# Five places for the first eight pieces of words, and no preparing step ahead of the first gated row

## The chip, the cores and the metric

The kernel runs on one core of one Trainium2 chip. The metric is the device time of one execution in microseconds (us). A profile comes from one execution, whose span is a little different from the timed runs.

## The reference

Two blocks stand behind each other, all in float32. The first is attention over hash buckets, with 4 batches, 8 heads, 768 tokens and 64 numbers a head. The second is a feed-forward block with a gate, on 3072 tokens of 512 numbers, with 1536 hidden ones.

```
q_bits = (q @ proj > 0);  k_bits = (k @ proj > 0)        # 6 bits each
mask   = bucket(q_bits)[:, None] == bucket(k_bits)[None, :]
scores = where(mask, q @ k.T / sqrt(D), -1e9)
attn   = exp(scores - max) / (sum + 1e-9)
x      = (attn @ v), heads side by side                  # (3072, 512)
out    = (silu(x @ w_gate) * (x @ w_val)) @ w_out
```

The weights w_gate, w_val and w_out come in as float64, and the kernel reads them as pairs of 32-bit words.

## The kernel before

**Attention.** Two heads make a pair, and a batch has four pairs. A pair is worked on in two half-units of 384 queries, and a half-unit in six units, one for each chunk of 128 keys. `score` multiplies queries and keys on TensorE (PE), adds the bits of the hash by a second product, and lets ScalarE (ACT) take the exponential (L458). `attend` (L469) multiplies the result with v. `add` (L483, L487) sums the exponentials on VectorE (DVE); `total` (L500, L508, L513) turns the sum into a reciprocal and spreads it by DMA from SyncE's queue (SP); `norm` (L520) applies it. `front` prepares the next pair: transposes of k and q (L377 on PE for the first pairs, L420 on DVE for later ones), and hash products (L394, L402), whose signs ACT takes (L387) and DVE scales (L389).

**Gated rows.** From the unit `LATE`, which is the first half-unit of batch 1, the feed-forward of the batch before runs in between: after the scores and `attend` of a half-unit PE works on one gated row. There are six such rows in a batch, numbered 0 to 5 here, and each has 14 steps: seven products of Strassen's scheme, each for gate (g = 0) and value (g = 1). They use three banks of PSUM, a, b and c, for each of the two, out of seven that scores and other products share in turn. A product is copied from its bank by ACT (L607) or added to a tile by DVE (L548); ACT takes the tanh (L530), DVE finishes gate (L531) and product (L535). Before row 0 DVE makes eight sums of the inputs (L548, `xc` and `xT`). In row 0 the products go in the order 0, 3, 1, 2, 4, 5, 6, so the product that DVE adds at once (number 3, called A12) is the second one. After the six rows come the output products (`po`, L544, with sums at L548).

**Words.** The float64 weights arrive in 36 pieces of 512 KB: 24 of the gate and value weights in turns of four, and 12 of w_out. Each needs a *place* in SBUF until it is narrowed to float32. The list `homes` says which: `early` and `middle` are two sets of four places inside `hid`, the tile which later holds the hidden values of the rows; `beside` and `late` are inside `room`, which also holds weights, sums and some exponentials; `None` takes one of two own buffers (`words`). `load_words` issues the DMA of a piece (L263, from GpSimd's queue, POOL, the first two from SP), a few pieces ahead of the one being narrowed:

```
        for i in range(len(words), len(pieces)):
            if i - done > (6 if 8 <= i < 28 else 4):
                break
```

A DMA into a place which was used before waits, in the issuing queue, until the piece before it there is narrowed; what stands behind it in the queue waits as well.

**Preparing steps.** Narrowing a piece takes two ACT instructions (L278, L279, called by `scale_to`, ahead of need) and three DVE instructions: L292, L294 and L297. Each DVE instruction is one *preparing step*. After four pieces of the gate and value weights `form` takes four steps more (L326, sums of Strassen's scheme), and writes blocks to DRAM from POOL's queue (`ram`, L318, L320, L329). `bring` (L308, POOL) reads a block back for the row that needs it, in two parts. After the last piece, twelve steps (L349) combine the rows of w_out. There are 144 steps from piece 0 on. `prepare_on(n)` takes n of them, and the main loop says where: so many after each half-unit, and then so many for each step of a gated row, with `part` counting the steps of the row:

```
        prepare_on(4)
        if half == 1 and n >= NP:
            total(n)
        prepare_on(0 if LATE - NCH <= u <= LATE else 3)
        ...
            if part < 9:
                prepare_on(size)
```

The order of every engine's instructions is the order in which the program writes them. Nothing is moved by a scheduler.

Of the kernel before, what the change touches and what calls it, by code (L numbers as in the profile page):

```python
# [18 lines left out]
def kernel(  # L19
# [175 lines left out]
    def part(size, at=None, **dims):  # L195
        at = taken[0] if at is None else at
        taken[0] = at + size
        if len(dims) == 0:
            return room[:, at : at + size]
        ((axis, length),) = dims.items()  # L200
        return room[:, at : at + size].rearrange(f"p (n {axis}) -> p n {axis}", **dims)
# [42 lines left out]
    def as_words(t):  # L244
        return t.bitcast(I32).rearrange("p (f w) -> p f w", w=2)

    spots = [hid[:, half, m].rearrange("p f q -> p (f q)") for half in range(2) for m in range(2)]
    early = [as_words(t[:, 0 : 2 * PIECE]) for t in spots]
    middle = [as_words(t[:, NFP // 2 * HQ : NFP // 2 * HQ + 2 * PIECE]) for t in spots]
    late = [as_words(part(2 * PIECE, at=stage_at + i * 2 * PIECE)) for i in range(4)]  # L250
    beside = as_words(part(2 * PIECE, at=down_at + 8 * BL))
    turn = [None] * 2 + [beside]
    homes = [(early + middle)[i % 8] for i in range(12)]
    homes += middle + turn + middle + turn + late + turn + late[:3]

    def load_words(done, queue=nc.gpsimd):
        for i in range(len(words), len(pieces)):
            if i - done > (6 if 8 <= i < 28 else 4):
                break
            words[i] = homes[i]  # L260
            if words[i] is None:
                words[i] = wraw.tile([P, PIECE, 2], I32, tag="words", name="words")
            queue.dma_start(words[i].rearrange("p f w -> p (f w)"), pieces[i][1])  # L263
# [18 lines left out]
    def scale_ahead():  # L282
        scale_to(min(progress["piece"] + 4, progress["scaled"] + 1))
# [70 lines left out]
    def prepare_on(n):  # L354
        for _ in range(n):
            next(preparing, None)
# [84 lines left out]
    LATE = NP * 2 * NCH  # L441
# [5 lines left out]
    def score(u):  # L447
        n, half, c = units[u]
        qs = slice(half * HQ, (half + 1) * HQ)
        ks = slice(c * P, (c + 1) * P)  # L450
        sc = [bank("sc")[:, 0:HQ] for _ in range(2)]
        for x, start in ((T, True), (bits, False)):
            for h in range(2):
                rows = slice(h * D, (h + 1) * D)
                nc.tensor.matmul(sc[h], x["k", n][rows, ks], x["q", n][rows, qs],  # L455
                                 start=start, stop=not start)
        for h in range(2):
            nc.scalar.activation(weights(u)[:, h, 0:HQ], sc[h], AF.Exp, scale=SCALE)  # L458

    def attend(u):  # L460
        n, half, c = units[u]
        b, pr = pairs[n]
        a = weights(u)
        if c == 0:
            av[n] = av_ps.tile([P, 512], FP32, tag="av", name="av")
        ps = av[n]
        width = AW if half == 0 else HQ
        for h in range(2):
            nc.tensor.matmul(ps[h * D : (h + 1) * D, 0:width], raws["v", n][:, h, c, :],  # L469
                             a[:, h, 0:width], start=c == 0, stop=c == NCH - 1)  # L470
        if c == NCH - 1:
            if half == 0:
                xT[b, pr] = xp.tile([P, S], FP32, tag="xT", name="xT")
                mean[n] = att.tile([P, 1], FP32, tag="e", name="e")
                nc.scalar.activation(mean[n], ps[:, HQ : HQ + 1], AF.Copy, scale=EPS)
            nc.scalar.copy(xT[b, pr][:, half * HQ : (half + 1) * HQ], ps[:, 0:HQ])

    def add(u):
        n, half, c = units[u]
        a = weights(u)  # L480
        if c == 1:
            acc[n, half] = att.tile([P, 2, HQ], FP32, tag="acc", name="acc")
            nc.vector.scalar_tensor_tensor(out=acc[n, half], in0=weights(u - 1)[:, :, 0:HQ],  # L483
                                           scalar=S * EPS / P, in1=a[:, :, 0:HQ],
                                           op0=ALU.add, op1=ALU.add)
        elif c > 1:
            nc.vector.tensor_tensor(acc[n, half], acc[n, half], a[:, :, 0:HQ], op=ALU.add)  # L487

    def total(n):

        b, pr = pairs[n]

        ps = av_ps.tile([P, 512], FP32, tag="av", name="sum") if b == 0 else bank("sum")
        t = [acc.pop((n, half)) for half in range(2)]
        for h in range(2):
            for half in range(2):
                g = (2 * h + half) * BLOCK
                nc.tensor.matmul(ps[g : g + BLOCK, 0:HQ], ones, t[half][:, h, :],  # L500
                                 start=True, stop=True)
        if b == 0:
            space = wo.rearrange("p f m -> p (f m)")
            space = space[:, n % 2 * 3 * HQ : (n % 2 + 1) * 3 * HQ].rearrange("p (x q) -> p x q", q=HQ)
            r, t = space[:, 2, :], space[:, 0:2, :]
        else:
            r, t = t[1][:, 0, :], t[0]
        nc.vector.reciprocal(r, ps[:, 0:HQ])  # L508
        for half in range(2):
            for h in range(2):  # L510
                g = (2 * h + half) * BLOCK
                for at in (h * D, h * D + BLOCK):
                    nc.sync.dma_start(t[at : at + BLOCK, half, :], r[g : g + BLOCK, :])  # L513
        waiting.append(lambda: norm(n, t))
        if pr == NP - 1:
            push_ffn(b)
# [200 lines left out]
    def prepare_pair(count):  # L717
        for _ in range(count):
            rest.extend(f for f in steps.pop(0)() or [] if f)

    def finish(todo):
        while todo:
            todo.pop(0)()
# [5 lines left out]
    for u in range(0, N, NCH):  # L729
        n, half, _ = units[u]  # L730
        gating = u >= LATE
        if u == MOVE:
            progress["late"] = True
            for t in late_ring:
                nc.gpsimd.memset(t[:, :, HQ:AW], 1.0)
        for c in range(NCH):
            score(u + c)
            if u == 0 and c in (0, 1, 2, 4):
                prepare_pair(1)
                finish(rest)  # L740
            if c == 1 and half == 0 and 0 < n <= NP:
                total(n - 1)
            if c:
                add(u + c)
        if n <= NP:
            finish(waiting)
        if not gating and half == 0:
            steps = front(n + 1)
        if not gating and u > 0:
            prepare_pair(2)  # L750
        for _ in range(1 if u else 2):
            scale_ahead()
        for c in range(NCH):
            attend(u + c)
        if not gating:
            scale_ahead()
        if half == 1 and n + 2 < len(pairs):
            load(n + 2)
        if not gating:
            prepare_pair(2 if u > 0 else 4)  # L760
        finish(first)
        finish(rest)
        prepare_on(4)
        if half == 1 and n >= NP:
            total(n)
        prepare_on(0 if LATE - NCH <= u <= LATE else 3)
        if not gating:
            continue
        chores = []
        if n + 1 < len(pairs):  # L770
            if half == 0:
                steps = front(n + 1)
                chores = [None, steps.pop(0), None, steps.pop(0)]
            else:
                chores = [None, steps.pop(0)]

        credit += 14 if n < 2 * NP else 15.75
        end = True
        part = 0
        while atoms and (credit > 0 or not end):  # L780
            size, atom, end = atoms.pop(0)
            credit -= size
            atom()
            part += size
            if part >= 11 or u + NCH == N and part >= 6:
                finish(waiting)
                if u + NCH == N:
                    finish([first.pop(0) for _ in range(min(2, len(first)))])
            if part < 9:
                prepare_on(size)  # L790
            if 6 < part < 11 or u == LATE and part > 10:
                scale_ahead()
            for _ in range(size):
                if chores:
                    step = chores.pop(0)
                    chores.extend(step and step() or [])
        while chores:
            step = chores.pop(0)
            chores.extend(step and step() or [])
# [34 lines left out]
```

## Time and profile before

| | |
|---|---|
| Timed runs | 1016.1, 1016.38, 1018.3 us; median 1016.38 |
| Span of the profile | 1016.9 us |
| PE busy | 1005.1 us (99%) |
| DVE busy | 574.4 us (56%) |
| ACT busy | 418.1 us (41%) |
| POOL busy | 98.8 us (10%) |
| Data moved by DMA | 106.21 MB, mean 104 GB/s |
| Landing of a piece into `hid` (POOL; w_val) | 8.1 us median |
| Landing of a piece into `words` (w_out) | 9.2 us median |
| Landing of a piece into `room` (w_out) | 6.6 us median |

Busy time is the time in which an engine had an instruction in work; PE's ends are modelled, so a busy PE can still be a slow one. For that the profile has a row for the clock that PE was granted, in tenths of full speed. The preparing steps are all done by some 300 us, so the first third of the span holds everything that the change touches. In the chain of waits, the work that ended last, PE has 88% and DVE 6%.

### The profile page before, as it was taken

The page shows a single profiled execution, that of the slowest core. Times are in us where ns is not written, and L with a number is a line of the kernel's source. Part 1 is how long each engine was busy: PE and PEld are TensorE (multiplying, and loading weights), DVE is VectorE, ACT ScalarE, POOL GpSimd, SP SyncE. Part 2 cuts the span into 40 slices and gives each one's busy share as a digit, 9 for nine tenths or more (in the row PEclk, how much of TensorE's full clock was granted, in tenths as well). Part 3 has the DMA queues.
Part 4 walks back from the last instruction along what each step waited for, and adds up shares of the span by engine and source line. Part 5 has one row for each costly group of instructions (what it writes and reads, how often), then busy time and mean ns, then how long its engine had stood idle before and what let it go on. Part 6 is the DMA issues. An engine that isn't in the chain of part 4 may idle for free.

```text
span 1016.9 us, 12485 instructions
## 1 busy us (share of the span) xinstructions
PE 1005.1 (99%) x4597; PEld 605.6 (60%) x4597; DVE 574.4 (56%) x919; ACT 418.1 (41%) x921; POOL 98.8 (10%) x192
## 2 busy tenths in 40 slices
PE   8999989999999999999999999999999999999998
PEld 3444445555566775555557676555555787555687
DVE  4688888878884425645455462454657351434421
ACT  5677646565542413535342422535435211222200
POOL 3121233211000000000000000000000000111000
PEclk9899999999999999999999999999999999999999
DMA  8477676665323123333421303332222011323001
GB/s 275 113 255 227 177 227 197 200 225 146 102 73 68 37 51 94 91 97 104 104 76 39 78 16 93 99 88 84 73 75 86 22 37 49 107 83 114 31 26 37
DMA packets 120029, 106.21 MB, mean 104 GB/s; under 512 B 89024, under 2 KB 103360, under 8 KB 119968
## 3 DMA queue, kind: packets, MB, share of 16 engines
q0 software_dynamic: 19104, 73.28, 22.0%
q1 hardware_dynamic: 100064, 31.94, 13.6%
q8 instruction: 36, 0.59, 0.3%
q10 hardware_dynamic: 800, 0.20, 0.1%
q14 instruction: 25, 0.20, 0.1%
HBM read 81.79 MB, written 17.30 MB: 97 GB/s over the span
## 4 chain that ended last, share of the span: by engine, by line
PE 88%; DVE 6%; DMA 2%; SPq 2%; issue 1%; ACT 1%; DVEq 0%
PE up L544 41%; PE po L544 22%; PE sc L455 12%; PE av L469 10%; SPq L513 2%; DMA qraw<-in_q_dram 1%; DVE acc L487 1%; PE sum L500 1%; DVE wo L508 1%; PE hps L402 1%; DMA wo<-wo 1%; DVE room L294 1%; PE hps L394 1%; DVE room L326 0%; DVE room L292 0%
## 5 line engine op out<-in xcount | busy, mean ns | idle before, releaser
L544 PE MATMUL up<-xT,room 128*128 128x384 f32 x768 | 263.7, 490 | 0.4 <-DVE xT L520 0.4
L544 PEld LDWEIGHTS up<-xT,room 128*128 128x128 f32 x768 | 144.1, 190 | 110.4 <-issue 15.5
L544 PE MATMUL up<-xc,room 128*128 128x384 f32 x576 | 199.2, 490 | 2.9 <-ACT c L607 2.9
L455 PE MATMUL sc<-qT,kT 64*128 64x384 f32 x768 | 162.2, 499 | 0.1
L544 PEld LDWEIGHTS up<-xc,room 128*128 128x128 f32 x576 | 110.4, 192 | 80.0 <-ACT c L607 3.5
L548 DVE TENSOR_TENSOR c<-c,up 128x384 f32<-128x384 f32 x72 | 39.8, 553 | 179.4 <-PE up L544 178.5
L487 DVE TENSOR_TENSOR acc<-acc,A 128x768 f32<-128x768 f32 x128 | 122.7, 958 | 15.4 <-ACT A L458 2.5
L308 POOL DMA_DIRECT2D room<-ram x96 | 52.1, 543 | 700.8 <-PE up L544 692.4
L458 ACT ACTIVATE A<-sc 128x384 f32<-128x384 f32 x256 | 105.2, 501 | 5.6 <-PE sc L455 5.6
L455 PEld LDWEIGHTS sc<-qT,kT 64*128 64x128 f32 x768 | 67.9, 189 | 52.4 <-issue 44.8
L679 ACT COPY o<-po 128x256 f32<-128x256 f32 x48 | 17.9, 372 | 196.1 <-PE po L544 196.0
L469 PE MATMUL av<-A,vraw 128*64 128x384 f32 (+1 forms) x512 | 88.2, 486 | 0.0
L530 ACT ACTIVATE th<-c 128x384 f32<-128x384 f32 x72 | 37.6, 523 | 115.9 <-DVE c L531 84.0
L548 DVE TENSOR_TENSOR o<-o,po 128x256 f32<-128x256 f32 x36 | 15.2, 421 | 113.2 <-PE po L544 84.1
L458 ACT ACTIVATE room<-sc 128x384 f32<-128x384 f32 x128 | 54.4, 492 | 38.1 <-PE sc L455 37.7
L544 PE MATMUL po<-wo,hid 128*128 128x256 f32 x288 | 66.9, 382 | 0.0
L544 PE MATMUL po<-wo,room 128*128 128x256 f32 x288 | 66.3, 380 | 0.0
L544 PE MATMUL po<-room,hid 128*128 128x256 f32 x288 | 66.1, 380 | 0.0
L607 ACT COPY c<-up 128x384 f32<-128x384 f32 x72 | 34.4, 478 | 73.7 <-PE up L544 73.4
L455 PE MATMUL sc<-qb,kb 64*128 64x384 bf16 x384 | 64.6, 325 | 0.1
L469 PEld LDWEIGHTS av<-A,vraw 128*64 128x64 f32 x512 | 36.7, 137 | 46.0 <-issue 45.3
L483 DVE SCALAR_TENSOR_TENSOR acc<-room 128x768 f32<-128x768 f32 x32 | 30.4, 949 | 57.2 <-ACT room L458 57.0
(109 smaller groups left out, 1024.2 us busy)
## 6 DMA issues: line engine op xcount, KB each, us to landing
room<-ram POOLq DMA_DIRECT2D x48, 512.0 KB, 4.7
room<-ram POOLq DMA_DIRECT2D x48, 384.0 KB, 3.9
vraw<-in_v_dram SPq DMA_DIRECT2D x16, 384.0 KB, 3.4
ram<-room POOLq DMA_DIRECT2D x12, 512.0 KB, 5.8
out_dram<-o SPq DMA_DIRECT2D x48, 128.0 KB, 1.7
hid<-in_moe_w_val_dram POOLq DMA_DIRECT2D x11, 512.0 KB, 8.1
qraw<-in_q_dram SPq DMA_DIRECT2D x48, 96.0 KB, 3.1
acc<-acc SPq DMA_DIRECT2D x96, 48.0 KB, 1.9
```

Source lines behind the costliest of these rows:

```text
L308: nc.gpsimd.dma_start(places[k % 2][:, PARTS[go], :], ram[k % NG][:, PARTS[go], :])
L455: nc.tensor.matmul(sc[h], x["k", n][rows, ks], x["q", n][rows, qs], start=start, stop=not start)
L458: nc.scalar.activation(weights(u)[:, h, 0:HQ], sc[h], AF.Exp, scale=SCALE)
L469: nc.tensor.matmul(ps[h * D : (h + 1) * D, 0:width], raws["v", n][:, h, c, :], a[:, h, 0:width], start=c == 0, stop=c == NCH - 1)
L483: nc.vector.scalar_tensor_tensor(out=acc[n, half], in0=weights(u - 1)[:, :, 0:HQ], scalar=S * EPS / P, in1=a[:, :, 0:HQ], op0=ALU.add, op1 ...
L487: nc.vector.tensor_tensor(acc[n, half], acc[n, half], a[:, :, 0:HQ], op=ALU.add)
L513: nc.sync.dma_start(t[at : at + BLOCK, half, :], r[g : g + BLOCK, :])
L530: nc.scalar.activation(th, g, AF.Tanh, scale=0.5)
L544: nc.tensor.matmul(ps, a, x, start=start and i == 0, stop=i == len(pairs_) - 1, skip_group_check=True)
L548: nc.vector.tensor_tensor(o, a, b, op=op)
L607: nc.scalar.copy(tile_of(g, spot), c)
L679: nc.scalar.copy(o, c)
```

## The change

Two things change. First, the list of places. The first eight pieces use five places (`early` and `beside`) in turn, where before they had eight; pieces 8 to 11 take `middle`, and so on with another order for all later ones. Six pieces ahead are now allowed for pieces 8 to 23, and no longer to 27. Second, the preparing steps: at the unit `LATE` none is taken ahead of the gated row, where before there were four, and inside that row they are taken when `part` is 6 to 13 and no longer when it is 1 to 8, so eight as before. PE's instructions and SP's keep their order. The four steps that are not taken then are made up for at the first output chunk of batch 0.

```diff
-    turn = [None] * 2 + [beside]
-    homes = [(early + middle)[i % 8] for i in range(12)]
-    homes += middle + turn + middle + turn + late + turn + late[:3]
+    homes = [(early + [beside])[i % 5] for i in range(8)] + middle
+    homes += [beside, None, None] + middle + [beside, None, None] + middle[:2]
+    homes += late[:2] + [beside, None] + late[2:] + [None] + late[:2] + [beside] + late[2:]

-            if i - done > (6 if 8 <= i < 28 else 4):
+            if i - done > (6 if 8 <= i < 24 else 4):

-        prepare_on(4)
+        prepare_on(0 if u == LATE else 4)

-            if part < 9:
+            if 5 < part < 14 if u == LATE else part < 9:
                 prepare_on(size)
```

## The prediction, on record before the changed kernel ran

> **What bounds the kernel now.** I read the page's busy shares first: PE is busy 1005.1 of 1016.9 us, so only what makes PE wait, or run slowly, can be won, and a clock row that is not 10 everywhere matters as much as a wait. The waits of PE alone come next:
>
> ```profile
> PE tps L377 <- DMA qraw<-in_q_dram: 3.6, 1, 3.6
> PE up L544 <- ACT c L607: 2.9, 1, 2.9
> ```
>
> Two single waits make most of what is not start or tail. The stretches around them show what follows each (columns after the stretch: its length, then busy us of PE, PEld, DVE, ACT, POOL, the granted clock, DMA share, GB/s):
>
> ```profile
> 21.60:25.10 3.50, 0.00 (x0) 0.02 (x1) 1.03 (x2) 1.64 (x4) 0.53 (x1) 0.82 1.13 326
> 25.10:30.70 5.60, 5.59 (x22) 3.40 (x24) 0.00 (x0) 2.31 (x6) 0.00 (x0) 0.50 0.71 217
> 134.00:136.80 2.80, 0.00 (x0) 0.00 (x0) 2.80 (x6) 1.68 (x5) 0.83 (x2) 0.95 0.82 262
> 136.80:141.00 4.20, 4.18 (x8) 2.40 (x9) 4.17 (x8) 2.60 (x5) 3.48 (x6) 0.63 1.05 271
> ```
>
> After each wait PE gets half a clock: 5.6 us at 0.50 is 2.8 us lost; the eight matmuls from 136.8 take 4.2 us where the eight from 143.6 take 2.7 us, 1.5 us lost. So the first place costs 3.56 + 2.8 = 6.4 us, the second 2.85 + 1.5 = 4.35 us.
>
> Why the first wait: the DMA answer for 17.5 to 20.5 us, by queue (packets, MB, share; q0 is POOL's, q1 SP's):
>
> ```profile
> q0 software_dynamic: 310, 1.12, 93.4%
> q1 hardware_dynamic: 295, 0.08, 11.2%
> ```
>
> Pair 1's q (SP, issued 13.07) lands 11.2 us later, at 24.98, because POOL issued six pieces of words (2 to 7, 512 KB each) from 11.69 to 14.86; q1 moves 0.66 MB only in 21.5 to 24.5, when q0 has drained.
>
> Why the second: the timeline of DVE and ACT before the stalled matmul.
>
> ```profile
> 130.21 0.69 DVE L297 CUSTOM_DVE_ANT_0 room<-hid,room 128x1024 uint16<-128x1024 uint16 x1
> 133.67 0.97 DVE L420 STREAM_TRANSPOSE qT<-qraw 128x768 f32<-128x768 f32 x1
> 134.57 0.52 DVE L548 TENSOR_TENSOR c<-c,up 128x384 f32<-128x384 f32 x1
> 135.12 0.52 ACT L530 ACTIVATE th<-c 128x384 f32<-128x384 f32 x1 [9.01 <-DVE c L548]
> 136.28 0.49 ACT L607 COPY c<-up 128x384 f32<-128x384 f32 x1
> 136.82 1.65 PE L544 MATMUL up<-xc,room 128*128 128x384 f32 x2 [2.85 <-ACT c L607]
> ```
>
> Six preparing steps (130.21 to 133.67) stand ahead of the sum at 134.57. ACT sits 9.01 us at the tanh of that sum, and behind it in ACT's queue stands the copy (136.28) that frees the bank PE wants.
>
> [...]
>
> **The change, part by part.** *Places.* Piece 4 goes beside, untouched and free at once; piece 5 now takes piece 0's place, 6 piece 1's, 7 piece 2's, so POOL waits for L297 of those (DVE ends them at 20.5, 22.4, 38.1). Ahead of q on q0 there are three pieces instead of six: 3 x 0.524 = 1.57 MB less, at 1.12 MB in 3 us (0.373 MB/us) 4.2 us less. q lands at 24.98 - 4.2 = 20.8. PE is ready for it at 21.55 (after the k transposes of 20.68). The scores that follow use pair 0, so need no copy of the new q. Wait and slow clock go: -6.4 us. Bounds: 0 if q gains nothing, -6.4 at best. Everything to the first gated row hangs on PE and SP events and moves along: PE has 12.00 of 12 us busy from 36 to 84, at about 12.0 us a half-unit (attends at 35.11 and 118.71, seven apart), so PE paces it although the chain of waits runs through DVE there.
>
> Pieces 7, 8, 9 stand behind the wait for piece 2 in POOL's queue (before: 8, 9 at 20.79 and 22.68). They are issued at about 32 once all is earlier; scaled by ACT at 53 or later, landing 6 to 9 us: hidden. The writes to ram behind them (L318, 40.33, waiting for piece 3's L297) are hardly later than now.
>
> *First gated row.* Six steps leave the place ahead of the sum: four (L297, L292, L294, L297) before the row, two in it. 133.67 - 130.21 = 3.46 us: the sum goes to 131.1, the tanh to 131.7, and the copies follow at 132.1, 132.5 and, once PE has made its product, 132.9, done 133.4. PE wants the bank at 133.9. Wait 0, no half clock: -4.35 us (PE ends the row at 141.7 to 141.9 instead of 146.3). But eight steps now lie in parts 6 to 13: 3 x L297 0.61, 2 x L292 0.45, 2 x L294 0.73, L326 0.70 = 4.9 us. I add DVE's queue up by start-to-start times of the trace (0.47 a sum or gate, 0.90 a transpose): two transposes, two sums and two gates (3.7) bring it from 130.2 to 133.9; four sums and five gates (9 x 0.47 = 4.2) and the steps' 4.9 to 143.0, and with 0.2 of waiting for a product the gate (L531) that frees bank a is done at about 143.3. The sum that PE needs at 139.1 is done at 136.2. Scores rotate over seven banks and come to that bank in the third unit, 1.7 us after they start: 141.7 + 1.7 = 143.4. It just fits: 0 to +1.5 us, I take 0.2. POOL waits in this row for pieces 13 and 14 (L297 at 134.5 and 136.8) to load 20 and 21; behind it stand the bring of 140.4 and block 3's writes to ram (four L318/L320, 141.2 to 144.2), then the other bring at 144.3, wanted by PE some 11 us into the next row (about 162): hidden.
>
> *Later rows.* Four steps stay behind to the end (136 against 140 of 144 at the last row of batch 0). Rows 1 and 2: DVE idles 1.89 and 1.10 us before the first sum; nine steps stand there as before, or 0.4 us more: 0. Row 3: now PE loses 1.0 us (scores 231.79 to 237.88 where others take 5.05), since a step (L292, 225.40) waits 1.91 us for ACT's L278. In the new order L297 stands there, whose data is ready: up to -1.0. Against it, piece 30 is asked for behind the bring at 223.1 and scaled at about 228.7, so 5.5 us, where such a load takes 6.6 (room) or 9.2 us (words): ACT may wait 1 to 4 us there, with the last tanh and the score exponentials behind it: up to +3. I take 0. First output chunk: four more L349 at 0.60, +2.4 us on DVE; the sum s1 at 299.70 to 302.65, its second half wanted at about 302.4: +0.3.
>
> Sum: -6.4 - 4.35 + 0.2 + 0.3 = -10.25 on the profiled span of 1016.9: 1006.65. The runs shown have a median of 1016.38, 0.5 under it: 1006.1, said as 1006.2.
>
> **Rivals.** *Only the start wins*: DVE, saturated in the first row, frees bank a late; a 3 us stall of the scores with half a clock after it gives the 4.35 back. For: DVE at the limit there. Against: the copies leave ACT early by any count. 1016.4 - 6.4 + 0.3 = 1010. *Only the row wins*: q still arrives after the pieces, say because v (384 KB on the same ring) takes its share, or DVE, which the chain shows from 43 to 131 us, absorbs the start. Against: the equal packet counts, PE's 12.00. 1016.4 - 4.35 + 0.5 = 1012.5. *Slower*: the pieces of w_out (24 to 26 in row 2, 28 to 30 in row 3) now enter POOL's queue after the sums of the block before, and ACT[...] stops at L278 with the exponentials behind it. With 5.5 us from asking to use, and landings up to 10.9 us (the longest of words in 150 to 235), each row would cost 10.9 - 5.5 = 5.4 us and 1.7 of half clock (3.4 us at half), 7.1 in all; two rows 14.2, less 10.2: +4, 1020.4. Break-even is a landing of 5.5 - 1.7 + 10.2/2 = 8.9 us in both rows. Against: the loads of row 2 are asked for 7 us ahead, and typical ones land in 6.6. *No effect of the places*: excluded as to order, since the instruction order shows POOL's waits on DVE from piece 5 on.
>
> **How the numbers follow.** Both gains 0.66, start only 0.13, row only 0.13, slower 0.05, the rest (gains nearly returned in rows 2 and 3) 0.03. About 0.2%, 2 us, is what a measurement of this kernel can tell from no change. Low end: -6.4 - 4.5 - 1.0 = -11.9, 1004.5. The high end takes in the start alone and most of the row alone: 1011.7. Faster 0.92, same 0.03, slower 0.05.
>
> **What would show it.** Right: q landing within some 8 us of its issue, no PE wait for it near 21.5, the clock 1.00 from 20 to 31 us, the scores of the second half-unit ending near 27.3 instead of 33.6. In row 0: L548 into c less than 1 us after the transpose that follows the xc sums, ACT's idle time before its tanh 9.0 - 3.5 = 5.5 us, no PE wait for the L607 copy, and eight matmuls of that product in 2.7 us. Wrong: q landing after 22 us; a PE gap in the scores behind row 0, ended by DVE's last gates; ACT waiting for a DMA at L278 in rows 2 or 3 with PE waiting in turn. A total above 1012 refutes the sum, whichever step failed; one under 1004 means a gain that I have not seen.

## The result, and the profile after

The changed kernel takes 1008.74 us (median of four runs, 1007.17 to 1009.61), the kernel before beside it on the same chip 1017.34 us (1016.10 to 1019.22). The ratio is 0.9912, with a 95% interval of 0.989 to 0.9934: faster by 8.6 us in the medians. The two profiled executions differ by more, 1016.9 - 1005.4 = 11.5 us of span. Why these two differ is a result of its own, told below.

The head of the page of the changed kernel, and then its waits of PE (us in total, times, longest):

```profile
span 1005.4 us, 12486 instructions
PE 999.8 (99%) x4597; PEld 603.9 (60%) x4597; DVE 574.7 (57%) x919; ACT 417.4 (42%) x921; POOL 98.7 (10%) x192
PEclk9999999999999999999999999999999999999999
```

```profile
PE idle L134 <- DVE kb L131: 1.3, 1, 1.3
PE av L469 <- DVE wo L508: 0.4, 1, 0.4
PE up L544 <- DVE xT L520: 0.4, 1, 0.4
PE hps L394 <- ACT kT L380: 0.2, 1, 0.2
PE po L544 <- DVE room L548: 0.2, 1, 0.2
```

The waits for q (3.6 us) and for the copy of L607 (2.9 us) are both gone from this list, and no new one of that size is in it. DVE, ACT and POOL are busy as long as before.

The two stretches of the start, in the columns of the prediction (length; busy PE, PEld, DVE, ACT, POOL; granted clock; DMA share; GB/s):

```profile
21.60:25.10 3.50, 3.50 (x27) 2.06 (x28) 0.62 (x3) 3.50 (x11) 0.53 (x1) 1.00 0.60 202
25.10:30.70 5.60, 5.60 (x33) 2.45 (x31) 5.18 (x8) 4.96 (x12) 0.00 (x0) 1.00 0.81 199
```

PE is busy throughout at full clock, where before it stood still for 3.5 us and then ran 5.6 us at half. The queues in 17.5 to 20.5 us (packets, MB, share) show why:

```profile
q1 hardware_dynamic: 1478, 0.67, 91.1%
q0 software_dynamic: 14, 0.04, 3.7%
```

POOL's queue is nearly empty, since piece 5 is asked for only at 20.14, after the L297 that frees its place. SP's queue carries 0.67 MB in the 3 us that gave it 0.08 MB before. q comes in two loads, issued at 12.42 and 13.15. Each lands 7.5 us later, the second at 20.62, only 0.13 us before PE asks for it at 20.75. In the profiles of the other six executions with the new places (e0, e1, e4 to e7) PE has no wait for q either.

The first gated row, in the timeline of the changed kernel:

```profile
123.14 0.97 DVE L420 STREAM_TRANSPOSE qT<-qraw 128x768 f32<-128x768 f32 x1
124.04 0.52 DVE L548 TENSOR_TENSOR c<-c,up 128x384 f32<-128x384 f32 x1
124.15 5.33 PE L544 MATMUL up<-xc,room 128*128 128x384 f32 x16
124.59 0.52 ACT L530 ACTIVATE th<-c 128x384 f32<-128x384 f32 x1 [5.56 <-DVE c L548]
125.75 0.49 ACT L607 COPY c<-up 128x384 f32<-128x384 f32 x1
134.56 0.92 PE L455 MATMUL sc<-qT,kT 64*128 64x384 f32 x4
135.49 0.55 DVE L531 SCALAR_TENSOR_TENSOR c<-c,up 128x384 f32<-128x384 f32 x1
```

The sum (L548 into c) follows the transpose at once, ACT waits 5.56 us for it instead of 9.01, and PE runs sixteen matmuls in 5.33 us without a stop, 2.7 us for each eight. The last line is the gate that frees bank a: it ends at 136.0, and the third unit of scores wants the bank 1.7 us after 134.56, at 136.3. It fits by 0.3 us.

### The profile page after: what moved, and what is told of

Its sections match the earlier page's. It is cut to its first block, busy times and chain, and to the rows that moved or that the text cites. A ratio compares the mean times of both kernels' runs of the same rounds, so it can differ in the third digit from the quotient of the medians.

```text
span 1005.4 us, 12486 instructions
## 1 busy us (share of the span) xinstructions
PE 999.8 (99%) x4597; PEld 603.9 (60%) x4597; DVE 574.7 (57%) x919; ACT 417.4 (42%) x921; POOL 98.7 (10%) x192
## 4 chain that ended last, share of the span: by engine, by line
PE 89%; DVE 7%; SPq 2%; issue 1%; DMA 1%; DVEq 0%; ACT 0%
PE up L544 42%; PE po L544 21%; PE sc L455 12%; PE av L469 10%; SPq L513 2%; DVE acc L487 1%; PE sum L500 1%; DVE wo L508 1%; PE hps L402 1%; DMA wo<-wo 1%; DVE room L294 1%; PE hps L394 1%; DVE room L326 0%; DVE room L349 0%; DVE xT L520 0%
## 5 line engine op out<-in xcount | busy, mean ns | idle before, releaser
L548 DVE TENSOR_TENSOR c<-c,up 128x384 f32<-128x384 f32 x72 | 39.8, 553 | 179.7 <-PE up L544 178.5
L548 DVE TENSOR_TENSOR o<-o,po 128x256 f32<-128x256 f32 x36 | 15.1, 421 | 111.6 <-PE po L544 82.4
L607 ACT COPY c<-up 128x384 f32<-128x384 f32 x72 | 34.4, 478 | 74.5 <-PE up L544 74.3
L544 PEld LDWEIGHTS po<-wo,hid 128*128 128x128 f32 x288 | 54.2, 190 | 12.0 <-issue 4.9
```

The costliest lines, as they stand in the source:

```text
L544: nc.tensor.matmul(ps, a, x, start=start and i == 0, stop=i == len(pairs_) - 1, skip_group_check=True)
L548: nc.vector.tensor_tensor(o, a, b, op=op)
L607: nc.scalar.copy(tile_of(g, spot), c)
```

## The experiments

All were run beside the kernel before: e0 to e3 on one chip (before: 1017.24 us median of 27 runs, 1014.85 to 1020.91), e4 to e7 on another (1016.98, nine runs, 1016.13 to 1018.91).

**e0_after: the changed kernel once more.** No edit.

> The changed kernel once more, beside the others. If the two gains of the profiled pair (6.4 us at the start, 4.4 in the first gated row, 0.7 in row 3: 11.5 of span) are what every execution has, the median is 11 to 11.5 us under the kernel before. If one of them comes and goes between executions, as the first timing of 8.6 us suggests, the runs scatter over 2 to 3 us and the median gain is 8 to 10 us.

Measured 1009.17 (six runs, 1008.18 to 1009.59), ratio 0.9912 (0.9894 to 0.9931). The result repeats. The gain of 8.1 us is that of the second case, but the runs scatter over 1.4 us and not 2 to 3: most of what comes and goes is in the kernel before, as shown below. The span is 1007.2, which is 1.8 us more than in the first profile: 0.5 of it lies ahead of the first `attend`, the rest in rows 3 and 4 (table below).

**e1_places: the places and the limit alone.** The preparing steps as before:

```diff
-        prepare_on(0 if u == LATE else 4)
+        prepare_on(4)
-            if 5 < part < 14 if u == LATE else part < 9:
+            if part < 9:
```

> The new list of places and the new limit alone, with the preparing steps where they were. Theory: the wait of PE for q and the half clock behind it go (6.4 us), the wait of 2.9 us in row 0 stays: median 6 to 6.5 us under the kernel before. Rival (VectorE, which the chain showed from 43 to 131 us, absorbs the start): 0 to 2 us, with the gain lost before 130 us.

Measured 1012.07 (1010.65 to 1012.92), ratio 0.9939 (0.9922 to 0.9957). The gain of the start is there alone: 5.2 us, less than the 6 to 6.5 that I expected. The edit holds the new places and the new limit together; from row 0 on this kernel neither gains nor loses (table below), so what it wins is the start. The wait of row 0 is back at 2.85 us, but in the profile no half clock comes after it (the granted clock is 1.00 from 125.4 to 135.6 us):

```profile
130.17 3.07 PE L544 MATMUL up<-xc,room 128*128 128x384 f32 x8 [2.85 <-ACT c L607]
```

Eight matmuls in 3.07 us, not 4.2.

**e2_steps: the preparing steps alone.** The other half of the diff, on the kernel before.

> The preparing steps of the first gated row alone, with the places as before. Theory: the wait for q at 21.5 us stays, the one in row 0 goes together with its half clock: 4.4 us faster, 3.5 to 5. Rival (the moved steps pay it back through VectorE's last gates in that row): 0 to 2 us, with a PE gap in the scores behind row 0.

Measured 1014.99 (22 runs, 1012.14 to 1018.65), ratio 0.9975 (0.9965 to 0.9984). Row 0 is won and the start is not. The 2.25 us (1.6 to 3.6 by the interval) are fewer than the 3.5 to 5 expected. Its trace loses 0.5 us in row 4 and 0.5 at the first output chunk, and a half clock behind the wait in row 0 is not in every run of the kernel before (the one of 1014.85 us has a mean clock of 1.000). PE's longest wait is again

```profile
PE tps L377 <- DMA qraw<-in_q_dram: 3.5, 1, 3.5
```

**e3_q_ahead: q on POOL's queue, ahead of the pieces.** The kernel before, with nothing of the change:

```diff
-    for name, queue in (("q", nc.sync), ("k", nc.gpsimd), ("v", nc.sync)):
+    for name, queue in (("k", nc.gpsimd), ("q", nc.gpsimd), ("v", nc.sync)):
```

> Places and steps as before, but q of the second pair is loaded from GpSimd's queue, between k and the pieces of words, so no piece stands before it on any queue. Theory (q is starved by the six pieces on the other queue, its place does not matter): PE's wait for q goes, about 6.4 us faster as with the places, less up to 1 us if piece 2, asked for 3 us later, holds ScalarE. Rival (it is the number of bytes in flight that delays q, whatever the queue): q still lands after 22 us and the gain is under 2 us.

Measured 1012.21 (1011.15 to 1014.09), ratio 0.9944 (0.9926 to 0.9962), 5.0 us where 5.4 to 6.4 were expected, and the same as e1 although all eight places are used as before. q is issued at 12.61, the pieces behind it from 14.24 to 17.4, and PE does not wait for q. So it was not the number of early pieces as such, nor their places, but that they held up q from the other queue. As in e1, row 0 keeps its 2.85 us wait, and here a half clock follows it (0.50 from 130.8 to 134.2 us):

```profile
129.99 4.54 PE L544 MATMUL up<-xc,room 128*128 128x384 f32 x8 [2.85 <-ACT c L607]
```

**e4_none_ahead: no step ahead of row 0, but inside it at the old parts.**

```diff
-            if 5 < part < 14 if u == LATE else part < 9:
+            if part < 9:
```

> The changed kernel, but with the row's steps at parts 1 to 8 as before, and still none ahead of row 0. Two steps stand ahead of the sum instead of none: it comes about 0.9 us later, the freeing copy ends near PE's need. Theory (VectorE's queue up to the sum decides): PE waits 0.3 us at most in row 0, and the time is within 0.5 us of the changed kernel; the end of the row has more room. Rival (the place inside the row matters as much): a wait over 1 us in row 0 and 1 to 3 us slower than the changed kernel.

Measured 1009.74 (1009.08 to 1010.14), ratio 0.9926 (0.9913 to 0.9938), 1.1 us over the changed kernel beside it (e7). I expected less. A wait of 0.34 us for the copy and about 0.3 us behind the next one remain; row 0 gains 3.5 us here and 4.5 in e7.

**e5_late_parts: four steps ahead of row 0, the rest at the new parts.**

```diff
-        prepare_on(0 if u == LATE else 4)
+        prepare_on(4)
```

> The changed kernel, but with four steps ahead of row 0 again, and the row's own at parts 6 to 13. The sum comes 2.5 us later than in the changed kernel. Theory: PE waits about 1.9 us in row 0 (2.85 less the 0.9 of the two steps moved), mostly without half a clock behind it; the late words of rows 3 and 4 and the 0.45 us at the first output chunk go, since no step stays behind. So 0 to 1.5 us slower than the changed kernel. Rival (none of the later losses comes from the four steps): 2 us and more slower, with rows 3 and 4 as in the changed kernel.

Measured 1010.48 (1010.20 to 1010.77), ratio 0.9933 (0.992 to 0.9947), 1.9 us over e7 where I expected 1.5 at most. PE waits again, for about the time foreseen:

```profile
129.87 3.07 PE L544 MATMUL up<-xc,room 128*128 128x384 f32 x8 [1.79 <-ACT c L607]
```

So the four steps ahead of the row are the larger part of row 0, and the two taken out of its first parts the smaller. But no step stays behind in e5, and with that the losses in row 4 and at the first output chunk are gone.

**e6_ask_sooner and e7_after_beside_e6.** In the changed kernel, ACT waits for late words:

```profile
218.70 0.69 ACT L278 ACTIVATE wo<-words 128x512 f32<-128x512 f32 x1 [1.46 <-DMA words<-in_moe_w_out_dram]
246.47 0.67 ACT L278 ACTIVATE wo<-room 128x512 f32<-128x512 f32 x1 [2.25 <-DMA room<-in_moe_w_out_dram]
```

POOL's timeline shows when the second of these, piece 35, was asked for:

```profile
239.12 0.53 POOL L308 DMA_DIRECT2D room<-ram  x1 [6.81 <-PE up L544]
239.65 0.53 POOL L263 DMA_DIRECT2D room<-in_moe_w_out_dram  x1
```

The `bring` waits 6.81 us for PE to free its block, and the load stands behind it. With four steps left behind, fewer pieces are narrowed by then, and the limit of four pieces ahead lets the load into the queue only behind this `bring`. In e5, where no step stays behind, ACT has no wait for words from 195 to 260 us. e6 lets one more piece ahead from 29 on:

```diff
-            if i - done > (6 if 8 <= i < 24 else 4):
+            if i - done > (6 if 8 <= i < 24 else 5 if i > 28 else 4):
```

> The changed kernel, with pieces from 29 on allowed one place further ahead, so that GpSimd's queue has the loads of pieces 30 and 35 ahead of a bring that waits for PE. Theory (in rows 3 and 4 ScalarE waits for these two pieces, 1.5 and 3.1 us, and PE loses 0.3 to 1.3 us behind it): no wait of ScalarE for words there, 0.8 to 1.6 us faster than the changed kernel, and a smaller scatter. Rival (PE loses this time to VectorE's four steps, words or not): no change beyond 0.3 us.

> The changed kernel on the same chip as the three above, as what they are compared with: 8 to 9 us under the kernel before, with a loss of 0.4 to 1.3 us of PE in row 4 in its profile if the late words are what varies between executions.

Measured: e6 1006.81 (1006.68 to 1007.40), ratio 0.9898 (0.9885 to 0.9912); e7, the changed kernel, 1008.61 (1008.02 to 1008.86), ratio 0.9914 (0.99 to 0.9928). e6 is the fastest kernel of the study, 1.8 us under the changed one, with ranges that don't touch (0.8 to 1.6 were expected). In e6 POOL asks for pieces 30 and 35 ahead of the two `bring` instructions:

```profile
207.70 0.53 POOL L263 DMA_DIRECT2D words<-in_moe_w_out_dram  x1
211.67 0.53 POOL L308 DMA_DIRECT2D room<-ram  x1 [3.44 <-PE up L544]
...
233.82 0.53 POOL L263 DMA_DIRECT2D room<-in_moe_w_out_dram  x1 [1.26 <-issue]
239.02 0.53 POOL L308 DMA_DIRECT2D room<-ram  x1 [4.67 <-PE up L544]
```

and of ACT's waits for words only this one is left:

```profile
218.38 0.68 ACT L278 ACTIVATE wo<-words 128x512 f32<-128x512 f32 x1 [0.88 <-DMA words<-in_moe_w_out_dram]
```

**Where each kernel stands.** In each profile I took the start of the first `attend` matmul of a half-unit, minus the same in the kernel before (us; negative is earlier). A difference between two columns is what the stretch between them gave:

| | after the start | before row 0 | after row 0 | row 3's scores | row 4's scores | after the first output chunk |
|---|---|---|---|---|---|---|
| after | -7.0 | -7.1 | -11.7 | -12.4 | -12.0 | -11.5 |
| e0 | -6.6 | -6.5 | -11.1 | -11.4 | -10.2 | -9.7 |
| e1 | -6.5 | -6.7 | -7.9 | -8.0 | -7.9 | -7.9 |
| e2 | 0.0 | +0.7 | -3.9 | -4.0 | -3.5 | -3.0 |
| e3 | -7.2 | -6.8 | -6.7 | -6.6 | -6.6 | -6.6 |
| e4 | -6.5 | -6.2 | -9.7 | -10.3 | -9.4 | -8.9 |
| e5 | -6.5 | -6.2 | -8.2 | -8.2 | -8.2 | -8.2 |
| e6 | -6.8 | -6.9 | -11.5 | -12.5 | -12.5 | -12.0 |
| e7 | -6.8 | -6.8 | -11.3 | -11.6 | -11.1 | -10.7 |

The first `attend` of all already differs by up to 0.7 us between executions (after -0.65, e3 -0.73, e7 -0.34, e1 -0.10). With that taken off, the start gives -6.4 in every kernel that has it. The +0.7 of e2 before row 0 is a single wait of PE for L389 at 89.7, at work that the change doesn't touch. From the last column to the end of the span 0.4 us are lost in e2 and at most 0.1 in the others.

## The same wait, with and without a half clock

e1 and e3 have the same wait of 2.85 us at the same place, yet lose 0.4 and 1.8 us in the eight matmuls after it (3.07 and 4.54 us for 2.7). In the clock record of before, 1.00 and 0.50 hold in turn for 17.07, 6.83, 105.81, 3.41 and 877.2 us: 5, 2, 31, 1 and 257 times 3.413. In that of after, 1.00 holds for 1000.1 us, 293 times 3.413. A stretch here is such a length of 3.41 us, counted from a change of the clock, and an edge is where one ends. Here are windows of about that length around the wait, in e1 (the same time cut in two ways) and then in e3 (columns as above):

```profile
125.40:128.80 3.40, 1.92 (x6) 0.77 (x5) 3.37 (x6) 0.34 (x1) 0.53 (x1) 1.00 0.63 186
128.80:132.20 3.40, 2.03 (x6) 1.06 (x7) 3.40 (x7) 3.40 (x9) 2.88 (x4) 1.00 0.94 261
127.30:130.80 3.50, 0.65 (x3) 0.49 (x3) 3.50 (x6) 2.34 (x6) 1.48 (x3) 1.00 0.81 244
130.80:134.20 3.40, 3.40 (x11) 1.78 (x10) 3.37 (x8) 1.98 (x4) 2.69 (x6) 1.00 1.15 299
```

```profile
127.30:130.80 3.50, 0.81 (x3) 0.55 (x4) 3.50 (x7) 2.51 (x6) 1.66 (x3) 1.00 0.87 230
130.80:134.20 3.40, 3.40 (x7) 1.83 (x6) 3.37 (x8) 1.78 (x4) 2.69 (x5) 0.50 1.16 302
```

In e3 nearly the whole wait lies in the first window (PE busy 0.81 of 3.50 us), and the next one is granted 0.50. In e1, over the same 127.30 to 130.80, PE is busy for even less, 0.65 of 3.50 us, and the 3.40 us after that are granted 1.00. So the idle time alone does not tell the two apart. The author's estimate is that an edge cut the wait of e1 in two, at about the 128.8 us between its first two lines, with PE busy for 1.92 and 2.03 of 3.40 us. As the clock does not change there, where the edges of e1 lie was not shown.

In before, the wait of row 0 lies in a stretch with PE busy for 0.89 of 3.42 us (133.08 to 136.50), and the wait at the start begins in one with 1.11 of 3.42 (20.44 to 23.86). Each was followed by a stretch at 0.50. In e2, with its wait of 3.48 us at the start, the clock is 0.82 in 21.60 to 25.10 and 0.50 in 25.10 to 30.70, as in before. In e5, after the wait of 1.79 us, the eight matmuls take 3.07 us, and all five runs have a mean clock of 1.000. Waits between 1.79 and 2.85 us were not measured.

At the start of before the half clock lasts two stretches. The wait reaches from the stretch 20.44 to 23.86 into the next, which is at half (23.86 to 27.27, 0.50) and has PE busy for 2.16 us, and the one after that is at half again (27.27 to 30.68, 0.50).

Counted back in steps of 3.413 from a change of the clock (23.86 us in before, 1004.63 in after), the first edge of the span lies at 3.38 us in before and at 1.11 in after, so the place of the edges differs between these two executions. That it decides whether a half clock follows the wait of row 0 is the author's estimate.

Every run lists its mean clock. One stretch at half is 3.41 x 0.5 = 1.7 us, 0.17% of a run: by this estimate a mean of 1.000, 0.998, 0.997, 0.995 and 0.993 stands for none to four of them. The 36 runs of the kernel before in these two sets:

| mean clock | runs | mean time, us |
|---|---|---|
| 1.000 | 1 | 1014.85 |
| 0.998 | 11 | 1016.29 |
| 0.997 | 13 | 1017.27 |
| 0.995 | 8 | 1018.66 |
| 0.993 | 3 | 1020.75 |

A step is 1.5 us on the average (5.9 in four). The mean is (11 + 26 + 24 + 12)/36 = 2.0 stretches at half, 3.0 us at 1.5 each. The profiled execution of before has a clock of 0.995 and took 1018.7 us: it had three, two at the start and one in row 0. Five runs of e2 have a mean of 0.996; its trace, which has this mean too, shows two stretches at the start (0.82 and 0.50 in the windows above), and the rest of this mean was not shown. The 14 runs of the changed kernel (the first four, e0, e7) all have 1.000. In e1, the two runs with a mean of 1.000 took 1010.7 on the average and the four with 0.998, or one stretch, 1012.4. That accounts for about 1.4 of the 2.9 us by which the profiled pair (-11.5) shows more than the medians (-8.6). The rest is that the first profile of the changed kernel fell on the fastest of its four runs, 1.6 us under their median.

## Why the prediction was right, and where it was not

*The start, -6.4.* Right in mechanism and, against the profiled execution, in size: -6.4 in every kernel that has it. e3 shows the cause by another way, since moving q alone has the same effect. But of its two terms only the wait looks steady (3.56 and 3.48 us in the two traces that have it, before and e2). The half clock (2.8) is what those executions had: of the 22 runs of e2, one has a mean clock of 1.000, eleven have 0.998, so one stretch at most, and ten less. Not all of these stretches need lie at the start. One reading was off without harm: q's first load, issued at 13.07, lands at 24.14, and it is the second, issued at 13.80, that takes 11.2 us to 24.98. The room that was foreseen (q at 20.8, PE ready at 21.55) came out at 0.13 us in the profile of the changed kernel.

*The first gated row, -4.35.* Right in mechanism: the sum, the tanh's idle time (5.56, foreseen 5.5), the copy and the eight matmuls stand where the prediction put them. The profiled pair gives -4.6 before row 3, as the copy after the one that PE waited for also comes in time (0.4 us in e1). Again the term "eight matmuls 4.2 instead of 2.7" is not certain: e1 lost 0.4 there, e3 1.8. By the times, the preparing steps are worth 1012.07 - 1009.17 = 2.9 us net of what they cost later. e2 against before gives 1017.24 - 1014.99 = 2.25.

*Row 0's tail, +0.2.* Within 0.3 us of a stall, and none came.

*Later rows, 0.* This step failed in part. Row 3 gave 0.1 us in e2 and 0.25 to 1.0 in the others in which steps stay behind, inside the bounds set for it. Row 4 was not looked at: the prediction followed piece 30 behind its `bring` and not piece 35 behind the next one. It cost 0.4 us in the profile of after, 1.2 in e0, 0.9 in e4, 0.5 in e2 and e7. In e0 the chain can be read line by line:

```profile
248.31 0.66 ACT L278 ACTIVATE wo<-room 128x512 f32<-128x512 f32 x1 [3.07 <-DMA room<-in_moe_w_out_dram]
...
249.96 0.56 DVE L531 SCALAR_TENSOR_TENSOR c<-th,c 128x384 f32<-128x384 f32 x1 [2.61 <-ACT th L530]
...
251.63 0.59 PE L455 MATMUL sc<-qT,kT 64*128 64x384 f32 x1 [0.30 <-DVE c L531]
```

ACT waits for piece 35, the tanh behind it is late, DVE's gate waits for that, and PE for the bank. This is the mechanism of the rival "slower", but a small part of its size: 0.4 to 1.2 us in one row, where the rival had 5.4 and 1.7 of half clock in each of two. The four steps left behind open it, as e1 and e5, which have none, show no loss in row 4; e6 closes it by the order of POOL's queue alone. ACT's wait for words tells the size in every execution in which steps stay behind (us, from the traces):

| | ACT's wait, row 3 | row 3 gives | ACT's wait, row 4 | row 4 costs |
|---|---|---|---|---|
| e6 | 0.88 | 1.04 | 0 | 0 |
| after | 1.46 | 0.69 | 2.25 | 0.41 |
| e4 | 1.51 | 0.61 | 2.73 | 0.89 |
| e0 | 1.80 | 0.25 | 3.07 | 1.21 |
| e7 | 1.83 | 0.33 | 2.34 | 0.48 |
| e2 | 2.10 | 0.09 | 2.33 | 0.47 |

In row 3 gain and wait add up to about 2 us. In row 4 the cost is the wait less 1.85 us, so here ACT can be held up for that long without loss. The gain of 1.0 that the prediction saw in row 3 is there when the words are nearly in time, and in the changed kernel late words take part of it back. That rows 3 and 4 together came near the 0 of the prediction in after (-0.7 + 0.4) is luck; in e0 they cost 1.0.

*First output chunk, +0.3.* +0.45 in every kernel in which four steps stay behind, and 0 in the others.

*The sum.* -10.25 gave a span of 1006.65. The four executions of the changed kernel have spans of 1005.4, 1006.8, 1007.1 and 1007.8: their median, 1006.95, is 0.3 us above the sum. The last step, from the span to a time, failed. The prediction took 0.5 off because the median shown was 0.5 under the span. But the time of a run stands 1.8 us above the span of the same execution (1007.17 beside 1005.4, 1018.7 beside 1016.9). So 1006.65 meant 1008.4, and 1008.74 was measured. The profiled run of before was then 2.3 us above the median of the three shown, with three stretches at half clock where two are usual. Carried to the usual run, the gain is 10.25 - 1.5 = 8.8, and 8.6 was measured.

*The rivals.* "Only the start" would be e1 and "only the row" e2. They were measured at 1012.1 and 1015.0, and together they make the whole: 5.2 + 2.25 = 7.4 of the 8.1 us of e0 in their set, within the width of the intervals.

*Left open.* Which share of the half clocks of before belongs to the start and which to row 0 over many runs, since only one execution of each kernel has a trace. Open, too, is where the edges lay in e1. Also open is why the words of row 4 are up to 0.8 us later for ACT in one execution of the changed kernel than in another (3.07 us in e0, 2.25 in after).

## What to carry to other kernels

A load that is wanted soon can be held up by bulk loads on another queue that are not wanted for a long time: delaying those (e1, 5.2 us), or putting the urgent one ahead of them (e3, 5.0 us), had the same effect here. In a queue that issues DMAs, look at what an issue stands behind: here a load behind a `bring` that waited 6.81 us for PE was asked for only after it, at 239.65 us, and asking one piece sooner won 1.8 us. Before a sum is made on a profile, compare the time and the mean clock of the profiled execution with those of the other runs, and count a half clock after a wait like the 2.85 us of row 0 as a chance (of the six runs of e1, two have a mean clock of 1.000 and four 0.998).

## What the runs showed of the hardware

No half clock came after a wait of 2.85 us of PE in e1 (1.00 from 125.4 to 135.6 us, eight matmuls in 3.07 us). After the same wait one came in e3 (0.50 from 130.8 to 134.2, 4.54 us) and in before (0.50 from 136.50 to 139.91, 4.2 us). The wait of 1.79 us in e5 left all five of its runs at a mean clock of 1.000. Most of the spread of the kernel before goes with the mean clock: 1014.85 us at 1.000, 1020.75 on the average at 0.993. The changed kernel, which has no such wait, has 1.000 and stays within 1007.17 to 1009.61 in all its 14 runs. In 17.5 to 20.5 us of before, the counts of packets were nearly equal, 310 of POOL's queue and 295 of SP's, and the bytes were not: 1.12 and 0.08 MB. SP's queue moved 0.67 MB in the same 3 us of after, where POOL's moved 0.04.
